# Six products that nothing reads on TensorE's way to the last V, and VectorE without its 52 leading increments

## The chip, the cores and the metric

The kernel runs on one core of a Trainium2 chip. The time is device microseconds of one execution. The kernel before takes 374.33 us, the median of three runs (374.31 to 374.35).

## The reference

One decode step of a gated block. A layer norm of x (2 rows of 448) feeds two branches: attention with a cache (16 query heads on 8 heads of keys and values, 4096 positions, 256 wide), and a bilinear feed-forward part whose output is a gate. All is float32.

```python
def _A_ref(x, k_cache, v_cache, wq, wo):
    ...
    scores = jnp.einsum("bhqd,bhkd->bhqk", q, k) * (Dh ** -0.5)
    p = _softmax(scores, axis=-1)
    o = jnp.einsum("bhqk,bhkd->bhqd", p, v)
    return (lambda x, *d: x.transpose(*d))(o, 0, 2, 1, 3).reshape(B, Sq, Hq * Dh) @ wo
...
x = A_x
xn = _layernorm(x, axis=-1)
s = _A_ref(xn, A_k_cache, A_v_cache, A_wq, A_wo)
g = _silu(_B_ref(xn, B_w_gate, B_w_up, B_w_down))
return x + s * g
```

The caches hold 2 x 8 pairs of K and V of 4 MB each, 128 MB together; with the weights the kernel reads 158.5 MB.

## The kernel before, in words

The work goes pair by pair: 16 pairs of a batch row and a K/V head, numbered 0 to 15. The names in the code are `START` = 6 (the first six pairs, written out), `LAST` = 14 (pairs 6 to 13 run in a loop of four turns on TensorE, two pairs to a turn) and the two last pairs, 14 and 15, written out again.

Every transfer is issued by SP into one of two big buffers, `ring` (V of pair i beside K of pair i+1, 8 MB) or into `slot` (weights). SP issues a transfer when TensorE has read what stood in the buffer. The last transfer is cut: V of pair 15 in three quarters and one quarter, and then the last eight blocks of the output weights (`wo2`) in pieces of 5, 2 and 1 blocks, so that each can be used when it lands. In the profile all of these are `ring<-last`.

For one pair there are, in order: `scores` (TensorE, 32 instructions, tile `s`), `peak` (VectorE, row maxima `m`), `peak_of_all` (TensorE transposes `m` into `sm`, VectorE takes the maximum `mx`), `exponential` (TensorE spreads `mx` back by a transpose, VectorE scales it, ACT takes the exponential into `p` and sums its rows into `su`), `turned` (VectorE transposes `p` into `pT`), and `values` (TensorE, 32 instructions, tile `o`, reading `pT` and V). For the last pair, 15, the turned `p` goes into the `slot` buffer, and its values go into a bank of `s`; in the profile that is `s<-ring,slot`.

`Flow` records every operation and then issues each engine's own in the order in which they were recorded, with the waits that the recorded regions need. So the order of lines in `gated_decode_block` is the order on each engine, and all operations carry line 227 in the profile. Only the increments have a line of their own, 155: `issue` puts 52 of them on a semaphore `lead` at the head of VectorE's program, before any operation; nothing waits for that semaphore, and its number marks the first of the range that SP clears at the end.

A product that nothing reads is in the kernel already. The loop calls it twice in the second pair of each turn, behind the softmax and ahead of the values:

```python
def hold(p):

    PE.matmul(bank("cb"), ident, p[:, 0], start=True, stop=True)
```

It multiplies 512 columns of `p` by the identity, at full width, into the bank `cb`. The compiler makes two matmul instructions of one float32 product.

The end of the kernel goes like this on TensorE: the scores of pair 14, the gathering of the loop's outputs, the scores of pair 15 (in two halves), parts of the output projection, the two transposes of the last softmax, the values of pair 14, the rest of the projection into `wide`, the sum of the exponentials' rows (`total`, tile `sm<-su,add_step`), the values of pair 15, a spread of `wide`, `combine` (tile `cb<-ob`) and the last projection from `wo2` (`project_last`, tile `s<-ring,oT`). ACT scales the two outputs into `ob`, VectorE multiplies by the gate and adds x, and SP stores the result.

Of the kernel before, what the change touches and what calls it, by code (L numbers as in the profile page):

```python
# [28 lines left out]
NS = HALF // SIDE  # L29
EPS = 1e-5  # L30
START = B * GROUPS
LEAD = 52


class Flow:
# [114 lines left out]

    def issue(self):
        nc = self.nc
        lead = nc.alloc_semaphore("lead")
        for _ in range(LEAD):
            nc.vector.sem_inc(lead)
        self.settle()
        mine = self.loop()
        sems, marks = {}, {}
        for op in self.ops:
            if op["wanted"]:  # L160
                assert "gate" not in op
                if op["lane"] not in sems:
                    sems[op["lane"]] = nc.alloc_semaphore(f"s{len(sems)}")
                op["step"] = 16 if op["dma"] else 1
                marks[op["lane"]] = op["mark"] = marks.get(op["lane"], 0) + op["step"]
        done = nc.alloc_semaphore("done")

        def await_all(engine, waits):
            waits = [(sems[o["lane"]], o["mark"]) for o in waits]
            while waits:  # L170
                gate = engine.wait_ge(*waits.pop(0))
                if waits:
                    gate.wait_op(*waits.pop(0), "sem-ge")

        def put(op):
            engine = self.engines[op["engine"]]
            await_all(engine, op["waits"][:-1])
            for gate, n in op["gates"]:
                engine.wait_ge(gate, n).then_inc(gate, -n)  # L179
            made = op["call"]()  # L180
            for o in op["waits"][-1:]:
                made.wait_op(sems[o["lane"]], o["mark"], "sem-ge")
            if "gate" in op:
                made.then_inc(op["gate"], 16 if op["dma"] else 1)
            elif op["wanted"]:
                made.then_inc(sems[op["lane"]], op["step"])

        store = self.ops.pop()
        for name, engine in self.engines.items():
            todo = [o for o in self.ops if o["engine"] == name]  # L190
            if name == "SP":
                for op in todo:
                    put(op)
                await_all(engine, store["waits"])
                store["call"]().then_inc(done, 16)
                engine.sem_clear(range(lead.num, done.num))
                engine.wait_ge(done, 16)
                engine.sem_clear(done)
            elif name == "PE":
                for op in todo:  # L200
                    if op["turn"] is None:
                        put(op)
                    elif op is mine[0][0]:
                        await_all(engine, self.ahead)
                        with nc.Fori(0, len(mine), engines=[mybir.EngineType.PE]):
                            for o in mine[0]:
                                put(o)
            else:
                for op in todo:
                    put(op)  # L210
# [20 lines left out]
def gated_decode_block(nc, x, first, vk, last0, last1, wq0, wqx, wdq, wo, wgu, out):  # L231
# [30 lines left out]
    def bank(name=None):  # L262
        return banks[name] if name else two()[:, 0]
# [36 lines left out]
    plan(f"k{LAST + 1} v{LAST}", last0, [0, ROW, 2 * ROW])  # L300
    plan(f"v{LAST + 1} wo2", last1, [0, 6144, ROW, *(ROW + i * D for i in (5, 7, 8))])
    issue(3)


# [167 lines left out]
    def place(i):  # L472
        g, b = divmod(i, B)
        n = HKV - 1 - GROUPS
        return b * GROUPS + g if i < START else START + b * n + g - GROUPS if i < LAST else i
# [6 lines left out]
    def peak_of_all(m):  # L482
        sm = bank("sm")
        PE.transpose(sm[:1, :128], m[:, 0:1], ident)
        mx = work["mx"]()
        DVE.tensor_reduce(
            mx, sm[:1, None, :128].rearrange("p o (c j) -> p o j c", c=NT).to_broadcast([1, NT, W, NT]),
            axis=AX.X, op=OP.max)
        return mx

    def exponential(i, s, m, mx):
        sm = bank("sm")
        PE.transpose(sm[:, 128:129], mx.rearrange("p c j -> p (c j)"), one)
        DVE.tensor_scalar(m[:, 1:2], sm[:, 128:129], -1.0 / 16, None, op0=OP.mult)
        p = work["p"]()
        ACT.activation(p, s, AF.Exp, bias=m[:, 1:2], scale=1.0 / 16, accum_out=su[:, place(i):place(i) + 1])
        return p

    def turned(p, pT):
        DVE.transpose(pT.rearrange("p h n -> p (h n)"), p.rearrange("p h n -> p (h n)"))  # L500
        return pT
# [8 lines left out]
    def total(lo, hi, add):  # L510

        sm = bank("sm")
        PE.matmul(sm[:, :hi - lo], add.rearrange("p a r j -> p (a r j)"), su[:, lo:hi], start=True, stop=True)
        DVE.reciprocal(over[:, lo:hi], sm[:, :hi - lo])
# [36 lines left out]
    def project(oT, first, lo, hi):  # L551
        for i in range(lo, hi):
            t = i % NT
            PE.matmul(wide[W * t:W * (t + 1), :D], heads(oT, i, first), loaded["wo"][:, i * D:(i + 1) * D],
                             start=i < NT, stop=i >= LATE - NT)
# [9 lines left out]
    oT2 = sbuf([128, 1, 2, REP, W], "oT2")  # L565
    s = scores(0, query_of(0), two())
    issue(2)
    for i in range(START):
        p = softmax(i, s)
        if i == 1:  # L570
            ffn_in()
        if i == 3:
            ffn_out()
        if i == 4:
            query(1)
        o = bank("o")
        values(i, p, o)
        s = scores(i + 1, query_of(i + 1), two())
        if i + 1 < START:
            issue(1 if i + 2 == START else 1 + (i + 1 in weights))  # L580
        DVE.tensor_copy(ob[:, place(i)], o)
# [10 lines left out]
    def hold(p):  # L592

        PE.matmul(bank("cb"), ident, p[:, 0], start=True, stop=True)
# [26 lines left out]
    ps = [turned(p, work["pT"]())]  # L621
    project(oT0, 0, 0, EARLY)
    m = peak(late)
    project(oT1, GROUPS, EARLY, EARLY + NT)
    mx = peak_of_all(m)
    p = exponential(LAST + 1, late, m, mx)
    ps.append(turned(p, slot()[:, :1024].rearrange("p (h n) -> p h n", h=2)))

    o = bank("o")
# [2 lines left out]
    t = work["h"]()  # L632
    ACT.copy(t, wide[:, :D])
    total(14, 16, add_step)
    ACT.activation(ob[:, 6], o, AF.Copy, scale=over[:, 14:15])

    o = bank()
# [63 lines left out]
```

## Time and profile before

| what | value |
|---|---|
| median of three runs | 374.33 us (374.31 to 374.35) |
| profiled execution | 374.74 us |
| its span, first to last instruction | 373.3 us |
| mean granted TensorE clock | 0.785 |
| busy: PE / DVE / ACT | 201.8 / 74.1 / 27.8 us |
| read from HBM | 158.54 MB, 425 GB/s over the span |

Times of rows are in microseconds from the start of the span, those marked ns in nanoseconds. PE is TensorE's matmul, PEld its load of weights, DVE VectorE, ACT ScalarE, SP the engine that issues transfers; a name with q is the engine's sequencer. `o<-ring,pT 128*32 128x512 f32 x32` reads: 32 instructions that write tile `o` from `ring` and `pT`, with 128 rows and 32 columns of weights and 128 x 512 elements moving. In brackets stands the idle time of the engine before the row and what ended it. The granted clock is the share of full speed that TensorE was given.

### The profile page before, as it was taken

The numbers are of one execution on the slowest core, as the hardware profiler recorded it, in microseconds if no ns is written. First come the engines' busy times: TensorE is split into PE (matmuls) and PEld (weight loads), VectorE is DVE, ScalarE is ACT, GpSimd is POOL, SyncE is SP. The second block draws the span as 40 slices with busy tenths as digits, with TensorE's granted clock in tenths as the row PEclk, the third lists the DMA queues.
The fourth block names the chain that finished last, engine by engine and source line by source line (L and its number), as shares of the span: only waits on it lengthen the run. The fifth ranks groups of instructions, "written<-read, shape, count | busy, mean of one in ns | idle before, by whom it ended". The sixth has DMA issues, their size and how long they took to land. (4 is left out here: it accounts for less than half of the span.)

```text
span 373.3 us, 3175 instructions
## 1 busy us (share of the span) xinstructions
PE 201.8 (54%) x1416; PEld 58.6 (16%) x1416; DVE 74.1 (20%) x114; ACT 27.8 (7%) x52; POOL 2.4 (1%) x14
## 2 busy tenths in 40 slices
PE   0782449081736084817403667285609470948976
PEld 0220112020101021202100122022202120212223
DVE  2103040103030013030310212122211221030620
ACT  1101010001021001010100000101000101010120
POOL 0100000000000000000000000000000000000000
PEclk9988596677686589886955959686957896776999
DMA  8999999999999999999999999999999999999995
GB/s 329 437 471 400 444 457 435 421 437 400 444 427 428 451 435 430 428 426 433 449 428 428 435 449 409 442 449 421 435 421 449 435 428 442 435 393 432 442 406 240
DMA packets 3921, 158.73 MB, mean 425 GB/s; under 512 B 566, under 2 KB 696, under 8 KB 840
## 3 DMA queue, kind: packets, MB, share of 16 engines
q1 hardware_dynamic: 3908, 158.59, 98.5%
q8 instruction: 8, 0.13, 0.1%
q10 hardware_dynamic: 4, 0.00, 0.0%
q14 instruction: 1, 0.01, 0.0%
HBM read 158.54 MB, written 0.06 MB: 425 GB/s over the span
## 5 line engine op out<-in xcount | busy, mean ns | idle before, releaser
L227 PE MATMUL o<-ring,pT 128*32 128x512 f32 x480 | 76.6, 797 | 101.0 <-DMA ring<-vk 54.2
L227 PEld LDWEIGHTS o<-ring,pT 128*32 128x32 f32 x480 | 19.0, 142 | 153.5 <-issue 97.1
L227 DVE COPY ob<-o 128x512 f32<-128x512 f32 x14 | 9.7, 692 | 168.4 <-PE o L227 168.4
L227 ACT ACTIVATE p<-s,m 128x1024 f32<-128x1024 f32 x16 | 17.8, 1113 | 303.1 <-DVE m L227 303.1
L227 PE MATMUL s<-ring,qT 128*32 128x512 f32 x256 | 30.8, 622 | 1.1 <-DVE qT L227 1.1
L227 PE MATMUL s<-ring,qc 128*32 128x512 f32 x256 | 29.0, 592 | 0.0
L227 DVE TENSOR_REDUCE m<-s 128x1 f32<-128x1024 f32 x16 | 19.5, 1220 | 41.2 <-PE s L227 41.2
L227 DVE STREAM_TRANSPOSE pT<-p 128x1024 f32<-128x1024 f32 x15 | 18.7, 1245 | 19.1 <-ACT p L227 19.1
L227 PE MATMUL cb<-pT,ident 128*128 128x512 f32 x16 | 14.8, 1081 | 11.4 <-PEq L179 11.4
L227 PE MATMUL s<-slot,xnT 128*32 128x512 f32 (+1 forms) x96 | 14.6, 757 | 3.7 <-DMA slot<-wgu 3.7
L227 PE MATMUL sm<-ident,m 128*1 128x128 f32 x16 | 4.3, 270 | 21.0 <-PEq L179 12.9
L227 DVE TENSOR_REDUCE mx<-sm 1x128 f32<-1x512 f32 x16 | 10.9, 679 | 7.9 <-PE sm L227 7.9
L227 PEld LDWEIGHTS s<-ring,qc 128*32 128x32 f32 x256 | 9.0, 110 | 18.6 <-issue 18.6
L227 PEld LDWEIGHTS s<-ring,qT 128*32 128x32 f32 x256 | 8.2, 114 | 20.8 <-issue 20.7
L227 PE MATMUL sm<-one,mx 1*128 1x1 f32 x16 | 3.3, 209 | 12.3 <-PEq L179 6.9
L227 PE MATMUL s<-slot,hT 128*32 128x448 f32 x28 | 5.6, 911 | 4.4 <-DMA slot<-wdq 4.4
L227 PE MATMUL s<-slot,oT 16*32 16x384 f32 (+5 forms) x28 | 8.0, 521 | 0.0
L227 PEld LDWEIGHTS cb<-pT,ident 128*128 128x128 f32 x16 | 4.7, 324 | 15.8 <-issue 15.8
L227 PEld LDWEIGHTS sm<-ident,m 128*1 128x1 f32 x16 | 1.3, 79 | 34.8 <-issue 20.4
L227 PE MATMUL s<-ident,pT 2*128 2x2 f32 (+1 forms) x8 | 0.7, 203 | 10.7 <-DVE pT L227 10.7
L227 PEld LDWEIGHTS s<-slot,xnT 128*32 128x32 f32 x96 | 3.3, 137 | 12.9 <-issue 9.1
L227 PE MATMUL wide<-slot,oT 128*32 128x448 f32 x48 | 4.9, 539 | 0.0
(65 smaller groups left out, 58.2 us busy)
## 6 DMA issues: line engine op xcount, KB each, us to landing
ring<-last SPq DMA_DIRECT2D x2, 4096.0 KB, 26.7
slot<-wdq SPq DMA_DIRECT2D x1, 6720.0 KB, 45.6
slot<-wgu SPq DMA_DIRECT2D x1, 6272.0 KB, 33.7
slot<-wo SPq DMA_DIRECT2D x1, 5376.0 KB, 38.1
ring<-first SPq DMA_DIRECT2D x1, 4096.0 KB, 20.6
slot<-wq SPq DMA_DIRECT2D x1, 3488.0 KB, 11.2
ring<-last SPq DMA_DIRECT2D x1, 3072.0 KB, 21.4
ring<-last SPq DMA_DIRECT2D x1, 1120.0 KB, 24.1
```

Source lines behind the costliest of these rows:

```text
L227: self.flow.record(self.engine, lambda: method(out, *args, **kw), writes, reads, name == "dma_start")
```

## The change

VectorE's 52 increments go; the semaphore that marks the range to clear stays, under the name `first`. Six products are recorded for TensorE: one between the two transposes of the last softmax, one behind the second of them (both on `ps[0]`, the turned `p` of pair 14), and four between the sum of the rows and the values of pair 15 (on `ps[1]`, the turned `p` of pair 15). They write the bank `cb`, which `combine` writes anew later.

```diff
-LEAD = 52
...
     def issue(self):
         nc = self.nc
-        lead = nc.alloc_semaphore("lead")
-        for _ in range(LEAD):
-            nc.vector.sem_inc(lead)
+        first = nc.alloc_semaphore("first").num
         self.settle()
...
-                engine.sem_clear(range(lead.num, done.num))
+                engine.sem_clear(range(first, done.num))
...
     mx = peak_of_all(m)
+    hold(ps[0])
     p = exponential(LAST + 1, late, m, mx)
+    hold(ps[0])
     ps.append(turned(p, slot()[:, :1024].rearrange("p (h n) -> p h n", h=2)))
 
     o = bank("o")
...
     ACT.copy(t, wide[:, :D])
     total(14, 16, add_step)
+    for _ in range(4):
+        hold(ps[1])
     ACT.activation(ob[:, 6], o, AF.Copy, scale=over[:, 14:15])
```

## The prediction

> **What bounds the kernel now.** I read the chain that ended last, then the timeline of the last 20 us, then the granted clock by stretches, and only then the start, where the increments stand. The profiled execution took 374.74 us, of which the span is 373.3; the three timed runs have a median of 374.33 (374.31 to 374.35). I work out a shift on the profiled execution and add it to the median; the 0.41 us between them is taken to be the same for both kernels.
>
> The page's rows of slices, and the chain in order of time (start us, length us, what):
>
> ```profile
> PEclk9988596677686589886955959686957896776999
> DMA  8999999999999999999999999999999999999995
> ```
>
> ```profile
> 337.30 5.84 PE o L227 x32
> 343.14 1.72 PE s L227 x15
> 344.86 24.06 DMA ring<-last
> 368.92 0.04 issue
> 368.96 2.06 PE s L227 x64
> 371.02 0.02 issue
> 371.05 0.28 DVE gate L227
> ```
>
> The DMA engines are busy at nine tenths or more in all slices but the first and the last, and the chain runs through the last transfers until 368.92. So transfers set the end, and the work between 344.86 and 368.92 matters only where it uses up its slack. How much slack that is, the timeline of the tail says (start, length, engine, line, operation; in brackets the idle time before it and what ended it):
>
> ```profile
> 355.74 0.27 PE L227 MATMUL sm<-ident,m 128*1 128x128 f32 x1
> 356.05 0.68 DVE L227 TENSOR_REDUCE mx<-sm 1x128 f32<-1x512 f32 x1 [1.11 <-PE sm L227]
> 356.78 0.22 PE L227 MATMUL sm<-one,mx 1*128 1x1 f32 x1 [0.77 <-DVE mx L227]
> 356.93 3.64 PE L227 MATMUL o<-ring,pT 128*32 128x512 f32 x32
> 360.39 1.69 PE L227 MATMUL wide<-slot,oT 128*32 128x448 f32 x16
> 362.01 0.30 PEld L227 LDWEIGHTS sm<-su,add_step 128*128 128x128 f32 x2 [0.73 <-issue]
> 362.01 0.38 PE L227 MATMUL sm<-su,add_step 128*128 128x2 f32 x2
> ...
> 363.81 3.64 PE L227 MATMUL s<-ring,slot 128*32 128x512 f32 x32 [1.42 <-DMA ring<-last]
> ...
> 366.29 0.25 PEld L227 LDWEIGHTS s<-ring,slot 128*32 128x32 f32 x8 [0.60 <-DMA ring<-last]
> ...
> 367.27 0.38 PE L227 MATMUL s<-h,add_head 128*32 128x112 f32 x8
> 367.52 0.69 ACT L227 ACTIVATE ob<-s,over 128x512 f32<-128x512 f32 x1 [4.20 <-PE s L227]
> 368.26 0.65 PE L227 MATMUL cb<-ob,add_blocks 128*32 128x128 f32 x16 [0.62 <-ACT ob L227]
> 368.96 1.40 PEld L227 LDWEIGHTS s<-ring,oT 128*32 128x32 f32 x56 [0.33 <-DMA ring<-last]
> ...
> 370.58 0.16 PEld L227 LDWEIGHTS s<-ring,oT 128*32 128x32 f32 x8 [0.22 <-DMA ring<-last]
> 371.05 0.27 DVE L227 TENSOR_TENSOR gate<-s,gate 128x112 f32<-128x112 f32 x1 [1.76 <-PE s L227]
> ```
>
> Here is the point of the case. TensorE waits 1.42 us for the last V (the record of 363.81). From there on the chain V, ACT, combine, last projection is almost as late as the transfers: what is left of waiting behind it is 0.33 us at 368.96 and 0.22 us at 370.58, part of which is the ordinary distance between weight loads. So TensorE's slack is 1.42 us ahead of the last V and under 0.55 us behind it, about 0.4.
>
> **The change part by part.** First the price of one product. The loop holds the same product already, two in each of its four turns (eight, shown as 16 instructions, so one is two instructions). The timeline of one turn, and the same stretch in a table (stretch, length, busy PE, PEld, DVE, granted clock, DMA share, GB/s):
>
> ```profile
> 332.28 3.75 PE L227 MATMUL cb<-pT,ident 128*128 128x512 f32 x4 [2.86 <-PEq L179]
> ```
> ```profile
> 332.20:336.00 3.80, 3.72 (x4) 1.18 (x4) 0.00 (x0) 0.50 0.90 388
> ```
> ```profile
> L227 PE MATMUL cb<-pT,ident x16: 857/1061/1193, 216.3 to 335.0; 128*128 128x512 f32 x16
> ```
>
> Four instructions in 3.75 us are 0.94 each at a granted clock of 0.50, the last one's way out included. The tail runs at 1.00, from 341.80 on:
>
> ```profile
> 335.00:338.40 3.40, 2.13 (x10) 0.46 (x12) 0.00 (x0) 0.00 (x0) 0.00 (x0) 0.50 0.89 386
> 338.40:341.80 3.40, 3.40 (x20) 0.92 (x16) 0.00 (x0) 0.00 (x0) 0.00 (x0) 0.50 0.98 424
> 341.80:345.20 3.40, 3.40 (x36) 1.05 (x32) 0.69 (x1) 0.00 (x0) 0.00 (x0) 1.00 1.00 434
> 355.70:362.40 6.70, 5.92 (x56) 1.98 (x52) 2.08 (x3) 1.46 (x3) 0.00 (x0) 1.00 0.98 419
> 362.40:363.80 1.40, 0.00 (x0) 0.00 (x0) 0.17 (x1) 0.92 (x2) 0.00 (x0) 1.00 0.94 398
> 363.80:367.30 3.50, 3.49 (x36) 1.09 (x40) 0.00 (x0) 0.00 (x0) 0.00 (x0) 1.00 1.01 427
> ```
>
> At full clock 512 columns pass in 0.43 us: the 32 instructions of the last V stand four abreast, so they are eight passes, from 363.81 to the next record at 367.27 (3.46 / 8). Half of 0.94 is 0.47. I take 0.43 for an instruction and 0.86 for a product, with 0.47 and 0.94 as the upper end. [...]
>
> *The first product of the last softmax* stands between the transpose of the maxima (355.74) and that of their maximum (356.78), where TensorE idles 0.77 us for VectorE. It can begin when the transpose ends (356.01) or a little ahead of that end, and 0.86 us of work then ends at 356.8 to 356.9. So 0.77 of it is hidden by VectorE's reduction of 0.68, and about 0.1 is not. Behind it the last exponential starts 0.1 later; it ends long before it is needed. If that cover were gone, the product would cost all of its 0.86.
>
> *The second* stands behind the transpose of 356.78 and ahead of the values of pair 14 (356.93). There TensorE waits for nothing: the values follow in 0.15 us, since their weights are an earlier softmax's. What waits at that time is ACT, for the exponential, and TensorE does not. So the whole 0.86 is new work, 0.9 with the change of weights. The values, the projection and the sum of the rows (until 362.01 + 0.38 = 362.39) all move by 0.1 + 0.9 = 1.0, to 363.4.
>
> *The four products ahead of the last V* stand behind that sum in TensorE's order and ahead of the V products. Four at 0.86 are 3.4 us, from 363.4 to 366.8. The wait that was to hold them was 1.42 us long and has shrunk to 0.4. The V products then start at 366.8 instead of 363.81: 3.0 us later. The first three quarters of V have been there for 3 us by then, and the last quarter, for which a weight load waits now at 366.29, comes ahead of the products' end too. No transfer sets the start any more.
>
> *Behind it*, values (3.46), ACT (until 368.21), combine and projection move by 3.0, less what they waited for: transfers that ended at 368.9 and 370.5 are now long there. That gives back at most 0.33 + 0.22, and I take 0.4, since weight loads have some distance anyway. The end moves by 3.0 - 0.4 = 2.6 us. Queued behind the products on TensorE are exactly these instructions; VectorE and SP have only the gate and the store left, which follow it.
>
> *The 52 increments* stand at VectorE's head. The line's view, the timeline and the page's part on queues in the stretch 10.5 to 13 show:
>
> ```profile
> L155 DVEq EVENT_SEMAPHORE  x52: 21/21/21, 0.8 to 5.5; - x52
> ```
> ```profile
> 7.32 0.61 DVE L227 TENSOR_REDUCE st<-p 2x1 f32<-2x448 f32 x1 [7.32 <-DMA p<-x]
> ```
> ```profile
> q14 instruction: 1, 0.01, 0.8%
> ```
>
> They end at 5.5, and VectorE's first operation waits until 7.32 for x, which ACT's queue fetches. Their removal is worth nothing; the cover is the load of x, with 1.8 us to spare. The one instruction packet on q14 took 0.8% of 16 engines in 2.5 us, 0.32 us on one DMA engine. If it is VectorE's, it may move or vanish with 52 instructions fewer, worth 0 to 0.3 us, either way, on one engine of 16. I count 0.
>
> **Sum.** 0.1 + 0.9 + (3.4 - 1.4) - 0.4 gives about 1.0 + 2.0 - 0.4 = 2.6 us. The profiled execution would be 374.74 + 2.6 = 377.3, the median 374.33 + 2.6 = **376.9 us**. The unknown prices (0.94 for a product; 0 to 0.15 for each of three changes to weights of full width, half of the 0.30 of the two loads at 362.01; 0.3 to 0.55 given back) put it between +2.4 and +3.6.
>
> **The clock's place.** The head's values from 337.30 ran at clock 0.50 until 341.80, though TensorE was busy all the time from 338.40 on (rows above). Work that takes 4.5 us at half clock takes 2.25 at full clock, so TensorE's tail would be up to 2.25 us earlier were the clock up from 337.3, and 1.1 later were it up only at 344. The kernel before hides much of that in its 1.42 us; the new one has no slack left, and its time follows the rise. One execution shows one place of it, between two neighbouring stretches of 3.4 us. I let it lie up to 2 us earlier and 2 us later, which is -1 and +1 on the time, and widen the range by that. [...]
>
> **The rivals.**
> - *The clock is up from 337.3 on (not slower).* The tail comes 2.25 us earlier, the wait for V is 1.42 + 2.25 = 3.67, and it takes 1.0 + 3.4 = 4.4 us of products less the 0.4 behind: +0.4, or 374.7, within the bound. It decides from a wait of about 3.3 us up. For it: the rise can fall elsewhere. Against it: in the profile the loop's products ran from 332.28 and the clock was still 0.50 at 341.8. Chance 0.04.
> - *A product costs half (not slower).* [...] Against it stand 0.94 for an instruction at half clock. [...] Chance 0.02.
> - *The increments were on the path (faster).* If x or the first issues really waited for VectorE's head, up to 5.5 - 0.8 = 4.7 us would go: 374.33 + 2.6 - 4.7 = 372.2. Against it: 1.8 us of idling for x behind them. It decides only if the first operation moves ahead of 7.3. Chance 0.02.
> - *The products run at half clock (slower still).* Six products cost 5.2 us more, about 382. Against it: 1.00 in all stretches from 341.80, and more work keeps TensorE busier. Chance 0.02.
>
> **How the numbers follow.** The forecast has a chance of 0.90. What a measurement can tell from no change is 0.2%, 0.75 us. Faster: 0.02 (the increments). Same: 0.06 (the first two rivals). Slower: 0.92. The range is 375.8 (the clock 1 us better) to 378.2 (dear products or a late clock); the forecast's own tails and the rivals leave out about 2 in 10.
>
> **What would show it.** In the new profile: a product tile cb from pT and ident at about 356.0 and 357.1, four more (of the slot tile) from 363.4 to 366.8 at clock 1.00; no DMA wait ahead of the last V's products, which start near 366.8; no DMA waits in the last projection; gate at 373.6; the chain that ended last runs through PE instead of DMA ring<-last from some 337 on. VectorE's first reduction stays at 7.3. I am wrong if the V products still wait for ring<-last, or if the six products take under 4 us together.

## The result, and the profile after

The changed kernel takes 375.48 us, the median of 15 runs (375.22 to 376.88), beside 374.41 us for the kernel before (15 runs, 374.21 to 375.27). The ratio is 1.0038, with a 95% interval of 1.0027 to 1.0048; the two medians alone stand as 1.0029 to 1. So it is slower, as forecast, but by 1.1 us between the medians and not by 2.6; the median lies under the range that was given (375.8 to 378.2).

The 15 times are not spread evenly. Nine lie at 375.22 to 375.68 and six at 376.70 to 376.88, and none between. The mean granted clock of each run sorts them in the same way: 0.776 to 0.795 in the lower nine, 0.763 to 0.773 in the upper six. The profiled execution, 376.88 us with a span of 375.4, belongs to the upper group. Its profile comes first, since its clock rises late (0.50 until 341.2, 1.00 from 341.4), as in the profile that the prediction worked with. The rows of slices and the chain that ended last (start, length, what):

```profile
PEclk9988697667786578957855959586859895968999
DMA  8999999999999999999999999999999999999993
```
```profile
336.92 5.79 PE o L224 x32
...
355.57 0.86 PE cb L224 x2
...
356.58 1.06 PE cb L224 x2
357.63 3.57 PE o L224 x32
...
363.02 3.54 PE cb L224 x8
366.56 3.62 PE s L224 x32
```

The 24 us of `DMA ring<-last` are gone from the chain. From 336.92 to 370.18 it is TensorE alone (behind that come ACT's `ob`, TensorE again and the gate), and the products (`cb` at 355.57, 356.58 and 363.02) are links of it. The timeline of the tail, with the same columns as before:

```profile
355.30 0.27 PE L224 MATMUL sm<-ident,m 128*1 128x128 f32 x1
355.41 1.02 PE L224 MATMUL cb<-pT,ident 128*128 128x512 f32 x2
356.36 0.22 PE L224 MATMUL sm<-one,mx 1*128 1x1 f32 x1
356.51 1.12 PE L224 MATMUL cb<-pT,ident 128*128 128x512 f32 x2
357.56 3.64 PE L224 MATMUL o<-ring,pT 128*32 128x512 f32 x32
...
362.64 0.38 PE L224 MATMUL sm<-su,add_step 128*128 128x2 f32 x2
362.88 3.68 PE L224 MATMUL cb<-slot,ident 128*128 128x512 f32 x8
366.50 3.64 PE L224 MATMUL s<-ring,slot 128*32 128x512 f32 x32
...
371.30 1.58 PEld L224 LDWEIGHTS s<-ring,oT 128*32 128x32 f32 x64
...
373.19 0.28 DVE L224 TENSOR_TENSOR gate<-s,gate 128x112 f32<-128x112 f32 x1 [1.22 <-PE s L224]
```

No bracket with `DMA ring<-last` is left, neither ahead of the last V's products (366.50) nor in the last projection (371.30). The gate stands at 373.19, 2.14 us later than before.

### The profile page after: what moved, and what is told of

It reads as the page before. It is cut to its first block, busy times and chain, and to the rows that moved or that the text cites. A ratio compares the mean times of both kernels' runs of the same rounds, so it can differ in the third digit from the quotient of the medians.

```text
span 375.4 us, 3146 instructions
## 1 busy us (share of the span) xinstructions
PE 209.1 (56%) x1428; PEld 60.6 (16%) x1428; DVE 74.1 (20%) x114; ACT 27.8 (7%) x52; POOL 2.4 (1%) x14
## 5 line engine op out<-in xcount | busy, mean ns | idle before, releaser
L224 PE MATMUL o<-ring,pT 128*32 128x512 f32 x480 | 77.9, 807 | 97.8 <-DMA ring<-vk 50.7
L224 PE MATMUL cb<-pT,ident 128*128 128x512 f32 x20 | 16.9, 987 | 11.4 <-PEq L176 11.4
L224 PE MATMUL s<-slot,xnT 128*32 128x512 f32 (+1 forms) x96 | 16.1, 825 | 4.1 <-DMA slot<-wgu 4.1
```

Of the source, the lines that this page charges most:

```text
L224: self.flow.record(self.engine, lambda: method(out, *args, **kw), writes, reads, name == "dma_start")
```

## The experiments

Each experiment is told by what it changes against the kernel named; products and increments are those of the change. The products' results are read by nothing, so every kernel here still computes the whole block.

**Increments alone.** Against the kernel before, only `LEAD` and its loop go.

```diff
-        for _ in range(LEAD):
-            nc.vector.sem_inc(lead)
```

> Only the 52 increments go; no product is added. Theory 'packet': the 8 KB instruction packet on q14 that stood at 11.3 us goes to about 185 us and off the DMA engine that lands last; the pieces of ring<-last land about 0.4 us earlier (last one at 370.1 instead of 370.5), and since transfers set the end here, the time falls by 0.3 to 0.4 us, to 374.0. Rival 'the increments are idle': last landing at 370.5 and the time within 0.1 us of the kernel before.

Measured: 374.38 us, ratio 1.0000 (0.9987 to 1.0012). The packet on q14 did move: the stretch 184 to 187 of this kernel's part on queues has the first row, and in its timeline the last load of the projection waits until 370.21 instead of 370.58.

```profile
q14 instruction: 1, 0.01, 0.6%
```
```profile
370.21 0.16 PEld L224 LDWEIGHTS s<-ring,oT 128*32 128x32 f32 x8 [0.22 <-DMA ring<-last]
```

So half of the 'packet' theory holds, where the packet goes, and the half that mattered fails: the median is that of the kernel before to 0.01 us, and ten of the twelve times lie at 374.19 to 374.65, as 29 of 35 of the kernel before do (374.06 to 374.63), where 0.3 to 0.4 us less were expected. The 0.37 us between the two profiles I put down to the spread of executions, which no run settles: the profiled execution of before (374.74) lay above that main group, and the clock rose at another place in it.

This profile shows something else, the kernel without the products in an execution whose clock was up early (the values of pair 13 take 3.64 us from 336.94, instead of 5.84):

```profile
356.16 5.34 PE L224 MATMUL o<-ring,pT 128*32 128x512 f32 x32 [1.52 <-DMA ring<-last]
...
363.43 3.64 PE L224 MATMUL s<-ring,slot 128*32 128x512 f32 x32
```

TensorE came to the last softmax 2.4 us sooner than in the profile of before (353.38 instead of 355.74), waited for V of pair 14, and passed that pair's values in 5.34 us instead of 3.64. So the time that it had won was spent again before the last V landed.

**The six products alone.** Against the kernel before, the products are added and the increments stay.

```diff
+    hold(ps[0])
     p = exponential(LAST + 1, late, m, mx)
+    hold(ps[0])
...
     total(14, 16, add_step)
+    for _ in range(4):
+        hold(ps[1])
```

> Only the six products are added; the 52 increments stay. Theory 'packet': 0.4 us slower than the whole change in like executions, since all of the tail starts 0.4 later: about 375.8 where the clock rises early, 377.2 where it rises late, +2.5 us in a profiled execution with the late rise. Rival 'the increments are idle': as the whole change, 375.4 and 376.8.

Measured: 375.53 us, ratio 1.0020 (1.0010 to 1.0031); eleven times at 375.2 to 375.8 and one at 376.66. The eleven, with a median of 375.53, lie where the lower group of the whole change does (375.22 to 375.68) and the one with its upper group, and not at the 375.8 and 377.2 of the 'packet' theory. The rival is right: the products are the change, and the increments do nothing that these times show. The ratio is lower than the whole change's, and the groups are mixed otherwise, with one of twelve in the upper one and not six of fifteen; whether the increments bear on that mix, so few times can't tell.

**The two early ones alone**, increments kept.

```diff
+    hold(ps[0])
     p = exponential(LAST + 1, late, m, mx)
+    hold(ps[0])
```

> Only the two products of the last softmax are added; increments stay, no products ahead of the last V. Theory 'the wait absorbs': they move the values of pair 14 by 0.8 to 1.0 us, the wait for the last V shrinks from 1.4 to about 0.5 us, and the time is that of the kernel before within 0.1 us. Rival 'they sit on the last softmax's path': +0.8 to +1.0 us.

Measured: 374.40 us, ratio 1.0000 (0.9986 to 1.0013). The median is as the wait's theory has it, but five of twelve times lie at 375.31 to 375.71, and the profiled execution (375.71), one of these, shows why. Its timeline, and stretches with the granted clock in the last column but two:

```profile
356.28 3.64 PE L227 MATMUL o<-ring,pT 128*32 128x512 f32 x32 [0.44 <-DMA ring<-last]
...
363.56 5.30 PE L227 MATMUL s<-ring,slot 128*32 128x512 f32 x32 [1.81 <-DMA ring<-last]
```
```profile
360.10:363.50 3.40, 1.64 (x18) 0.56 (x10) 0.17 (x1) 1.18 (x2) 0.00 (x0) 1.00 0.90 376
363.60:366.90 3.30, 3.30 (x16) 0.75 (x20) 0.00 (x0) 0.00 (x0) 0.00 (x0) 0.50 1.01 425
```

Here TensorE came to the last V 1.81 us early, the clock was down to 0.50 when V's products began, and they took 5.30 us instead of 3.64. In this execution that cost them 1.7 us. The other four of the group have no profile.

**The four late ones alone**, increments kept.

```diff
     total(14, 16, add_step)
+    for _ in range(4):
+        hold(ps[1])
```

> Only the four products ahead of the last V are added; increments stay. Theory 'path': 3.5 us of work in a wait of 1.4 us, less 0.4 us given back behind it: +1.7 us (376.1) where the clock rises near 341.5, and about 0 to +0.3 us (374.4 to 374.7) where it rises one window of 3.4 us earlier, as TensorE then comes 1.7 us sooner. Two groups of times. Rival 'the products cost their own time whatever the wait': +3.0 us and more.

Measured: 376.89 us, ratio 1.0046 (1.0030 to 1.0063). The median is higher than with all six products, since seven of twelve times lie in the upper group; the two intervals overlap. There are two groups, as expected, but at 375.11 to 375.69 (five) and 376.82 to 377.34, and the profile of the upper one (377.34) has the early rise (the values of pair 13 take 3.64 us from 337.11), which I had given to the lower one:

```profile
354.59 0.22 PE L227 MATMUL sm<-one,mx 1*128 1x1 f32 x1 [0.77 <-DVE mx L227]
356.33 5.34 PE L227 MATMUL o<-ring,pT 128*32 128x512 f32 x32 [1.52 <-DMA ring<-last]
```
```profile
353.50:356.80 3.30, 1.01 (x12) 0.39 (x12) 1.36 (x3) 1.21 (x2) 0.00 (x0) 1.00 0.96 415
357.00:360.20 3.20, 3.20 (x20) 0.76 (x16) 0.53 (x1) 0.00 (x0) 0.00 (x0) 0.50 1.05 453
```

TensorE waits twice (0.77 for VectorE, then 1.52 for the V of pair 14), the granted clock falls from 1.00 to 0.50, and the values of pair 14 take 5.34 us instead of 3.64. The last V's products start at 366.96, behind the four late ones. The two early products fill most of these waits, so in an execution with the early rise they save more than they cost (375.48 us with them in the next profile, 377.34 here). The lower group of this kernel has no profile.

**The changed kernel once more**, unchanged, for a profile of the lower group.

> The changed kernel itself, for a profile with the other place of the clock's rise. Theory 'clock': if its time is near 375.4, the granted clock rises at 335 to 338, the values of pair 14 start behind a wait for their transfer near 356.2 instead of at 357.6, and the last V's products start near 365.1; if it is near 376.8, the rise is at 340 to 342. Rival: a time near 375.4 with the rise at 340 or later.

It took 375.48 us. Its chain in order of time, and two stretches:

```profile
326.81 29.23 DMA ring<-last
356.04 0.04 issue
356.08 3.64 PE o L224 x32
359.72 1.50 PE wide L224 x16
361.22 0.31 PE sm L224 x2
361.54 3.54 PE cb L224 x8
365.08 3.62 PE s L224 x32
...
```
```profile
332.30:335.50 3.20, 3.13 (x4) 1.17 (x4) 0.00 (x0) 0.00 (x0) 0.00 (x0) 0.50 0.73 317
335.70:339.00 3.30, 2.38 (x22) 0.82 (x24) 0.00 (x0) 0.00 (x0) 0.00 (x0) 1.00 1.03 447
```

The clock is up from 335.7 on, TensorE is early, and the chain is another one: it comes out of the transfer of pair 14's V at 356.04, goes through the values and then through the four products (361.54) to the last V's products at 365.08. Neither of the early products is in it; the second lies ahead of the wait for that transfer, 0.46 us of which are left.

**Three products in the loop.** Against the changed kernel, so that TensorE is busy up to the values of pair 13.

```diff
             if i > first:
-                hold(p)
-                hold(p)
+                for _ in range(3):
+                    hold(p)
```

> The changed kernel with three products instead of two in the loop's second pair, so that TensorE is busy without a gap from about 331.8 to the values at 336.9. Theory 'clock': the rise of the granted clock then falls at 339 at the latest and mostly near 335 to 337, in every execution; the group of the changed kernel's times at 376.8 goes, and all of them lie at 375.2 to 375.8. Rival 'the two groups have another cause' (a transfer, an instruction packet): both groups stay, four in ten of the times near 376.8.

Measured: 375.43 us, ratio 1.0029 (1.0017 to 1.0041), and all six times at 375.33 to 375.76. Nothing but a product in each turn of the loop, far ahead of the change's place, has been added, and no time lies in the upper group. Six times are few: with six of fifteen in the upper group, none of six would come by chance about one time in 20. In the profile the values of pair 13 follow the loop's products without a wait and take 3.64 us instead of 5.79:

```profile
333.05 4.70 PE L224 MATMUL cb<-pT,ident 128*128 128x512 f32 x6 [2.86 <-PEq L176]
337.67 3.64 PE L224 MATMUL o<-ring,pT 128*32 128x512 f32 x32
```

**Eight late products.** Against the changed kernel, eight instead of four.

```diff
-    for _ in range(4):
+    for _ in range(8):
         hold(ps[1])
```

> The changed kernel with eight instead of four products ahead of the last V. Theory 'path': nothing hides any of the four new ones, each is two instructions of 0.43 us: +3.4 us in both groups, 378.8 and 380.2. Rival 'part of the wait is still there' (the transfer of the last V or its pieces end later than TensorE): +2 us or less.

Measured: 378.98 us, ratio 1.0135 (1.0119 to 1.0152), three times at 378.84 to 379.07 and one at 380.40. Four more products cost 3.5 us between the medians, and the same in both groups, the upper of which is a single time here:

```profile
361.45 7.11 PE L224 MATMUL cb<-slot,ident 128*128 128x512 f32 x16
368.50 3.64 PE L224 MATMUL s<-ring,slot 128*32 128x512 f32 x32
```

From 361.45 to 368.50 are 16 instructions in 7.05 us, 0.44 each. The rival, that a part of the wait was still there, is out.

**Two late products.** Against the changed kernel, two instead of four.

```diff
-    for _ in range(4):
+    for _ in range(2):
         hold(ps[1])
```

> The changed kernel with two instead of four products ahead of the last V. Theory 'path with the clock kept': where the clock rises early, TensorE is ready for the last V near 361.4 and V lands at 363.4, so 1.7 us of products fit, TensorE stays at full clock, and transfers set the end again: 374.0 to 374.4. Where it rises late, +1.7 us less than the whole change: 375.1. No execution at 376.8. Rival 'two products are too little activity': the clock falls in the wait and the last values run at half clock, 375.4 in the first group.

Measured: 374.52 us, ratio 1.0004 (0.9995 to 1.0013); nine of eleven times at 374.26 to 374.78, the others 374.91 and 375.17. In the profile the two products fill the wait and end as V lands:

```profile
361.66 1.96 PE L224 MATMUL cb<-slot,ident 128*128 128x512 f32 x4
363.61 3.64 PE L224 MATMUL s<-ring,slot 128*32 128x512 f32 x32
```

**Three in the loop, and two or one ahead of the last V**: the third product in the loop, combined with fewer late ones. The diff is that of the three products with `range(2)` or `range(1)` late ones.

> The changed kernel with three products in the loop's second pair and two, instead of four, ahead of the last V. Theory 'clock and path': the rise is early in every execution, both waits of the tail are filled without being overrun by more than 0.2 us, transfers set the end: all times at 374.2 to 374.7, none at 375.2 or above. Rival 'no room': the third loop product and the two late ones push the last V's products past its landing, +0.3 to +0.8 us in all executions.

> As the one before, with one product ahead of the last V. Theory 'clock and path': about 1.2 us of the wait for the last V is left empty, too short for the clock to fall, and the time is 374.1 to 374.5 in all executions, within 0.1 us of the kernel before's faster group. Rival 'the wait must be full': the clock falls near 363 to 367 in some executions, and a second group appears at 375.3 to 375.7.

Measured: 374.26 us with two (ratio 0.9996, 0.9987 to 1.0005; all eleven at 374.05 to 374.51) and 374.40 us with one (0.9997, 0.9988 to 1.0006; all eleven at 374.18 to 374.60). With one, 0.86 us of the wait are left, and no second group appears:

```profile
363.60 3.64 PE L224 MATMUL s<-ring,slot 128*32 128x512 f32 x32 [0.86 <-DMA ring<-last]
```

Neither is measurably faster than the kernel before: both intervals hold 1. What they show is that the cost of the change can be had back whole without taking all its products out, and that none of their 22 times lies where six of 35 of the kernel before did (375.15 to 375.66). Of all 87 times recorded of the kernel before beside the runs, nine lie at 375.1 or above; 22 without one would come by chance about one time in eleven, so that is a hint and no more.

## Why the prediction was right or wrong

**The price of a product** was right. Four late ones take 3.62 us from 362.88 to 366.50 (3.4 forecast), and 0.44 us an instruction in the eight; the granted clock is 1.00 from 362.9 to 366.5. The rivals of half a price and of half the clock are out: no run shows a product of this kernel in half of the 0.86 us.

**The two early ones** cost 0.0 and 1.05 us (0.1 and 0.9 forecast): the two transposes stand 1.06 us apart instead of 1.04, and the values 1.20 us behind the second one instead of 0.15.

**The sum on the profiled execution** nearly holds: the last V's products start 2.69 us later (3.0 forecast), 0.55 us is given back behind them (0.4), and the end moves by 2.14 (2.6). The chain through PE, the missing waits and the gate near 373.6 (373.19) came as described. Of the 0.46 us that are missing, 0.44 is the start: TensorE came to the tail at 346.06 instead of 346.50 in that execution. Most of that, 0.38, was there when the values of pair 13 began (336.92 instead of 337.30), and why isn't shown. The other 0.06 is the clock, which rose near 341.3 instead of 341.8:

```profile
337.90:341.20 3.30, 3.30 (x23) 0.79 (x19) 0.00 (x0) 0.00 (x0) 0.00 (x0) 0.50 1.01 437
341.40:344.00 2.60, 2.60 (x30) 0.81 (x24) 0.69 (x1) 0.00 (x0) 0.00 (x0) 1.00 0.96 416
```

**The clock's place** is the step that failed, and with it the range. I took the late rise of the one profile for the usual one, let it shift by 2 us, which was my estimate, and gave the early rise a chance of 0.04. In the changed kernel nine times of 15 lie in the group whose profile has the rise at 335.6. So the early rise is the usual case there, and the median is its time. The step from the profile to the median failed with it: the 0.41 us between them, taken to be the same for both kernels, are 1.40 in the changed one (376.88 and 375.48).

Nor was a shift by some 2 us seen. In the twelve profiles of all kernels the values of pair 13 take either 3.64 us (nine) or 5.49 to 5.84 us (before, after, and the six products alone). Of the nine, the rows of the clock in this document show the rise near 335.1 (two late products) and near 335.6 (the changed kernel once more); of the three, near 341.8 (before) and near 341.3 (after).

The profile of before could have told this. Its loop has the two products in four turns, and the values behind them took 3.64 us in two of these, and 5.76 and 5.84 us (the row of 337.30) in the others:

```profile
221.40 5.76 PE L227 MATMUL o<-ring,pT 128*32 128x512 f32 x32 [1.31 <-PEq L179]
...
260.03 3.64 PE L227 MATMUL o<-ring,pT 128*32 128x512 f32 x32
...
298.62 3.64 PE L227 MATMUL o<-ring,pT 128*32 128x512 f32 x32 [0.88 <-PEq L179]
```

The two products began at 216.34, 256.14, 294.19 and 332.28 in the four turns, and the clock rose near 225.7, 259.9, 297.4 and 341.8, that is 9.4, 3.8, 3.2 and 9.5 us later. So the same work had both places of the rise in one profile, two turns each, and the prediction went by the last turn alone.

**The rival of the early rise** had the mechanism and a wrong size: +0.4 us, 374.7, where 375.4 was measured. It let the tail come 2.25 us sooner. But the values of pair 14 read a transfer of their own, which lands at 356.04 in the profile of the lower group, so they can start at most 0.85 us ahead of the 356.93 of before. I had looked for waits in the tail as the profile had them and not for transfers that would end a wait if TensorE came sooner. Redone with that, after the runs, the sum comes out: values at 356.08, 5.46 us to the end of the rows' sum (as before, 362.39 - 356.93), 361.5, four products of 0.86 to 0.9, 365.1; that is 1.5 us behind the 363.6 at which the last V's products can start (the kernel with two late products), less 0.55 given back, about +1.0, and 1.1 was measured.

**The increments** were right at 0: their removal alone measures 1.0000, and VectorE's first operation stands at 7.23 and waits for x as before. The rival of a faster start is out.

```profile
7.23 0.61 DVE L224 TENSOR_REDUCE st<-p 2x1 f32<-2x448 f32 x1 [7.23 <-DMA p<-x]
```

**Left open**: whether the moved packet is worth anything below 0.1%, and what the lower group of the four late ones alone, and the kernel before's times at 375.15 to 375.66, look like in a profile. The latter lie where the two early ones alone have the last V's products at half clock, but that is only argued. Why the values of pair 13 began at 336.9 in one profile and at 337.3 in another is open too.

## What to carry to other kernels

Filler work in an engine's wait was free here only up to the wait's length at that place, in each of the ways in which the kernel came there: size it by the shortest wait that it meets, since all beyond it was paid in full (3.5 us for four products more, about 0.9 us each). Before you take a stretch of one profile for the rule, ask what the granted clock was in it and whether another execution can have its rise elsewhere (335.6 and 341.3 in two profiles of the changed kernel); if the stretch is one turn of a loop, look at its other turns; and when an engine might come sooner, look for the next transfer that it would then wait for.

## What the runs showed of the hardware that was not expected

In these runs the granted clock fell from 1.00 to 0.50 behind waits of under 2 us. In the two early products' kernel it fell behind a single wait of 1.81 us (1.64 us busy in the 3.4 us that ended with it), and in the four late ones' behind waits of 0.77 and 1.52 us (1.01 of 3.30). In the kernel before it stayed at 1.00 with 1.88 of 3.30 us busy, and in the kernel with two late products with 1.72 of 3.20, with a wait of 1.49 us in it:

```profile
362.30:365.60 3.30, 1.88 (x21) 0.60 (x25) 0.17 (x1) 1.02 (x2) 0.00 (x0) 1.00 0.97 410
```
```profile
335.20:338.40 3.20, 1.72 (x13) 0.50 (x16) 0.00 (x0) 0.00 (x0) 0.00 (x0) 1.00 1.04 451
```

In the profiles of before and after, neighbouring changes of the granted clock lie 3.41 us or a multiple of it apart (in the kernel before it is 1.00 until 24.34, 0.50 until 27.76 and 1.00 until 34.59). Each row is cut to fit into that distance, and the clock has one value in it. The two stretches that kept the clock were busy for 57% and 54%, and the two that lost it for 48% and 31%. The longest wait alone doesn't tell them apart: with 1.49 us the clock was kept, and a stretch of the changed kernel with waits of 1.43 and 0.86 us (1.11 busy of 3.30, from 249.2) lost it too. Nor does the busy share in every case. Near 21 us the kernel before lost the clock with 2.18 of 3.30 us busy (66%), and what is different there isn't shown:

```profile
21.00:24.30 3.30, 2.18 (x11) 0.65 (x13) 0.90 (x2) 0.00 (x0) 0.00 (x0) 1.00 0.99 427
24.40:27.70 3.30, 3.30 (x20) 1.08 (x16) 0.00 (x0) 0.00 (x0) 0.00 (x0) 0.50 0.87 377
```

Two stretches at 0.50 differ in what came behind them. The first row is the kernel before, whose clock stayed down behind it; the second is the kernel with two late products, whose clock rose at its end:

```profile
331.60:334.90 3.30, 2.62 (x3) 1.18 (x4) 0.53 (x1) 0.00 (x0) 0.00 (x0) 0.50 0.87 377
```
```profile
331.80:335.00 3.20, 2.74 (x4) 1.17 (x4) 0.31 (x1) 0.00 (x0) 0.00 (x0) 0.50 0.95 410
```

With 2.62 of 3.30 us busy (79%) it did not rise, with 2.74 of 3.20 (86%) it did. The work in both rows is the loop's two products, which begin at 332.28 and at 332.26, and the clock rises near 341.8 and near 335.1. So the same products at the same place were followed by either rise; in both rows they run up to the row's end. Two rows show no limit for the share, and what sets the place of the rise isn't shown. In the two profiles of the changed kernel the rises near 341.3 and 335.6 go with 376.88 and 375.48 us. That is how a kernel whose work is the same each time has two times 1.4 us apart.
